# Attention heads of the first two batches re-staged in a fused attention and two-layer kernel on one core

## The chip, the core and the metric

The kernel runs on one core of a Trainium2 chip. A core has a matrix engine (TensorE; PE in the profile, with its weight loads as PEld), a vector engine (DVE), an activation engine (ACT), a third elementwise engine (POOL) and a sync engine (SP) whose queue here issues every transfer. Each engine works through its own instruction stream in order; semaphores hold an instruction until what it reads or overwrites is ready. The metric is the device time of one execution in microseconds. Before the change it was 974.35 us, the median of three runs between 972.32 and 974.64.

## What is computed

For 8 batches of 8 heads with 576 positions of 64 numbers each, windowed causal attention: heads 0 to 3 see the last 32 positions, heads 4 to 7 every fourth of the last 128. Its output, 4608 tokens of 512 numbers, goes through two dense layers of width 2048 with a piecewise quadratic activation between them. In short:

```python
scores = (q @ k.T) / 8                      # per batch and head
scores = where(mask_plain or mask_dilated, scores, -1e9)
attn = exp(scores - max) / (sum(exp(scores - max)) + 1e-9)
x = (attn @ v) as [4608, 512]
h = x @ w_in                                # 512 -> 2048
g = where(h >= 1, h, where(h <= -1, 0, (h + 1)**2 / 4))
out = g @ w_out                             # 2048 -> 512
```

## The kernel before

Heads are numbered n = 8 * batch + head. Dilated heads are permuted on the host, so every head becomes six diagonal tiles of 96 queries by 128 keys. For one pair of heads the work is: scores on PE (tiles s), then one fused DVE instruction per tile that adds the mask, scales, negates and takes the row minimum (`reduce`, 12 for a pair), softmax on the tile c (in place, 96 x 768 for a head), six PE transposes per head (tiles t) copied by ACT and DVE into pt, and 24 small matmuls with the values (tiles o, 12 for each half). The values are stored as token columns in two parts: ACT writes the rounded part xh, DVE the residue xl (`store_x`).

The dense layers work in split precision. A block of 512 tokens is t, a block of 128 hidden units is f: `layer1(t, f)` is 12 matmuls of 512 columns into h, followed by a clamp on DVE, a square on ACT, a maximum on DVE, a rounding on ACT (gh) and a residue on DVE (gl); `layer2(t, f)` is 12 matmuls of 512 columns into four accumulators acc0 to acc3. The main loop runs over steps s = (t, f), 144 of them, with layer 1 of step s and layer 2 of step s - 2.

The weights come as 64-bit numbers. `fetch` transfers a block; `weights` turns it into a rounded part and a residue: two ACT instructions (one for w_out), one or two on DVE (the shift of wo_raw, the combination wi_m or wo_m), an ACT rounding and a POOL subtraction. `behind(marks, ...)` lets the preparation of a block begin only after an ACT and a DVE instruction named by the marks. In step s the blocks wo s and wi s + 3 are prepared, behind the activation of step s - 2.

The attention stands in three places. The first batch (heads 0 to 7, four pairs) is computed ahead of the loop; its `softmax_first` subtracts the row extreme of the whole head on POOL, takes one exponential of 768 columns on ACT, and on DVE sums the rows, takes the reciprocal and multiplies. The second batch (heads 8 to 15) is put into slots of the loop, two slots per step: slot 2s stands between layer 1 and layer 2 of step s, slot 2s + 1 behind layer 2. Its `softmax` uses six exponentials per head on ACT, each with the bias and the row sum in the instruction, and multiplies on POOL. Pair n starts at slot u = 7 (n - 8) / 2 with scores at u and u + 1, transposes at u + 5 and u + 6, values at u + 7. So the values of one pair and the first scores of the next fall into the same slot. From head 16 on another form is used, from slot 27; the change leaves that part alone.

The order on PE and on SP is the order in which the code is written. On DVE, ACT and POOL a list scheduler with an engine model sets the order; `tc.high_priority(offset=...)` moves instructions ahead in its list. PSUM gives h two banks, the attention two banks (tag "att"), the accumulators four; while the accumulators are unused, heads below 8 take the four acc banks in turn for scores and transposes (`bank`). Some buffers of late weight blocks hold operands of the first batch, so their transfers cannot start before these are used up.

Of the kernel before, what the change touches and what calls it, by code (L numbers as in the profile page):

```python
# [19 lines left out]
F32 = mybir.dt.float32  # L21
# [4 lines left out]
ALU = mybir.AluOpType  # L26
# [16 lines left out]
def body(ctx, tc, q, k, q2, k2, v, mask, eye, w_in, w_out, out):  # L43
# [105 lines left out]
    def bank(n):  # L149

        if n >= H:
            return "att", 2
        turn[0] += 1
        return banks[(turn[0] - 1) % len(banks)]
# [23 lines left out]
    def scores_pair(n, t0, t1):  # L178
# [24 lines left out]
        for m, sv in zip(pair, svs):  # L203
            for t in range(t0, t1):
                which = (0 if t == 0 else 2) if plain else t % 3
                reduce(m, t, (sv[:, t - t0], msk[:, which]))
# [34 lines left out]
    def softmax(n):  # L241
        c, st = heads[n]["c"], heads[n]["st"]
        for t in range(NQ):
            nc.scalar.activation(  # L244
                out=c[:, t],
                in_=c[:, t],
                func=AF.Exp,
                bias=st[:, 0, t : t + 1],
                scale=-1.0,
                accum_out=st[:, 1, t : t + 1],  # L250
            )
        nc.vector.scalar_tensor_tensor(  # L252
            out=st[:, 1], in0=st[:, 1], scalar=EPS, in1=st[:, 1], op0=ALU.add, op1=ALU.max
        )
        nc.vector.reciprocal(out=st[:, 2], in_=st[:, 1])  # L255
        nc.gpsimd.tensor_tensor(  # L256
            out=c, in0=c, in1=st[:, 2].unsqueeze(2).broadcast_to([QT, NQ, 128]), op=ALU.mult
        )

    def softmax_first(n):  # L260

        c, st = heads[n]["c"], heads[n]["st"]

        def spread(a):
            return a.unsqueeze(2).broadcast_to([QT, NQ, 128])

# [3 lines left out]
        nc.vector.scalar_tensor_tensor(  # L270
            out=st[:, 1], in0=st[:, 1], scalar=EPS, in1=st[:, 1], op0=ALU.add, op1=ALU.max
        )
        nc.vector.reciprocal(out=st[:, 2], in_=st[:, 1])
        last["dve"] = nc.vector.tensor_tensor(out=c, in0=c, in1=spread(st[:, 2]), op=ALU.mult)  # L274
# [46 lines left out]
    def store_x(src, t, c, dst):  # L321
        xh, xl = xtile(t)
        last["act"] = nc.scalar.copy(out=dst(xh[:, c]), in_=src)
        last["dve"] = nc.vector.tensor_tensor(  # L324
            out=dst(xl[:, c]), in0=src, in1=dst(xh[:, c]).bitcast(F32), op=ALU.subtract
        )
# [43 lines left out]
    def layer1(t, f, cs=range(NC), bank=("h", 2)):  # L370
# [13 lines left out]
        if cs[-1] < NC - 1:  # L384
# [5 lines left out]
        nc.vector.tensor_scalar(  # L390
            out=y, in0=hp, scalar1=-1.0, scalar2=1.0, op0=ALU.max, op1=ALU.min
        )
        nc.scalar.activation(out=y, in_=y, func=AF.Square, bias=half_t, scale=0.5)  # L393

        activated = nc.vector.tensor_tensor(out=hp, in0=hp, in1=y, op=ALU.max)  # L395
        copied = nc.scalar.copy(out=gh, in_=hp)  # L396
        if t == 0:
            last["g", f] = copied, activated
        nc.vector.tensor_tensor(out=gl, in0=hp, in1=gh.bitcast(F32), op=ALU.subtract)  # L399
# [57 lines left out]
    for n in range(H, native, 2):  # L457
        u = 7 * (n - H) // 2
        place(u, lambda n=n: scores_pair(n, 0, 4))
        place(u + 1, lambda n=n: (scores_pair(n, 4, NQ), after_pair(n)))  # L460
# [32 lines left out]
    def pair(n):  # L493
        scores_pair(n, 0, 4)
        scores_pair(n, 4, NQ)
        softmax_first(n)
        softmax_first(n + 1)
# [23 lines left out]
    with tc.manual_schedule(engines={mybir.EngineType.PE, mybir.EngineType.SP}):  # L521
# [28 lines left out]
        early_values(6)  # L550
        behind(second, ("wi", 3))
# [3 lines left out]
        for s in range(len(steps) + lag):  # L555
            if s == 1:
                for f in range(9, NF):
                    fetch(f, w_in, "wi")
                    fetch(f - 2, w_out, "wo")
                fetch(NF - 2, w_out, "wo")  # L560
                fetch(NF - 1, w_out, "wo")
# [78 lines left out]
```

## Time and profile before

| what | value |
|---|---|
| median of 3 runs | 974.35 us |
| the profiled execution: its own time | 970.9 us |
| its span, first to last instruction | 968.9 us |
| mean granted PE clock | 0.978 of full |
| DVE, ACT, POOL busy | 738.7, 479.4, 231.4 us |
| from 200 us on | PE busy all but a few us |
| PE busy from 0 to 200 us | 167.6 us of 200 |

Span and waits come from one execution taken by the hardware profiler. A line of a timeline view gives start, duration, engine, code line, operation, output<-input, shape and, in brackets, how long the engine had been idle and what ended that. A line of the view of the chain of waits gives start, length and the work on the path that ended last. A line of the view of stages gives the busy time of each engine in a stretch, the granted PE clock, the share of the DMA engines and their rate. Durations in a timeline include a tail in which the next instruction already runs: successive starts are closer than the durations. The lines that matter are shown in the prediction.

### The profile page before, as it was taken

How to read it: one execution, taken by the hardware profiler on the slowest of the kernel's cores; microseconds unless marked ns; L12 is line 12 of the kernel's file. 1: busy time of each engine (PE TensorE's matmuls, PEld its weight loads, DVE VectorE, ACT ScalarE, POOL GpSimd, SP SyncE). 2: the span in 40 equal slices, each digit the busy share in tenths (PEclk: the TensorE clock that was granted, in tenths of full speed). 3: DMA queues.
4: the chain of work that ended last, by engine and by line, in shares of the span. 5: the costliest groups of instructions: out<-in, count | busy, mean ns of one | idle time of the engine just before them, and what ended most of it. 6: DMA issues, size and time to landing. Idle time of an engine off the chain costs nothing.

```text
span 968.9 us, 14398 instructions
## 1 busy us (share of the span) xinstructions
PE 930.3 (96%) x4822; PEld 751.9 (78%) x4822; DVE 738.7 (76%) x2043; ACT 479.4 (49%) x1291; POOL 231.4 (24%) x148
## 2 busy tenths in 40 slices
PE   6779978999999999999999999999999999999997
PEld 5657767888777888878888888888788888888886
DVE  7888666988898898989898889898988743334333
ACT  2677765555565555545555555555555432222222
POOL 3344333222222222222222222222222200000000
PEclk8779999999999999999999999999999999999999
DMA  9674100322232222322232223211322010001001
GB/s 348 239 275 156 43 1 26 111 67 68 68 90 84 59 58 64 110 68 67 67 111 67 67 66 94 60 64 57 109 68 83 1 44 1 0 1 44 1 1 44
DMA packets 31017, 73.85 MB, mean 76 GB/s; under 512 B 3520, under 2 KB 3808, under 8 KB 30944
## 3 DMA queue, kind: packets, MB, share of 16 engines
q1 hardware_dynamic: 30944, 72.94, 23.1%
q8 instruction: 38, 0.62, 0.3%
q14 instruction: 35, 0.29, 0.1%
HBM read 63.49 MB, written 9.44 MB: 75 GB/s over the span
## 4 chain that ended last, share of the span: by engine, by line
PE 82%; DVE 9%; ACT 6%; issue 2%; DMA 1%; SPq 0%; POOL 0%; ACTq 0%; DVEq 0%; POOLq 0%
PE h L377 37%; PE acc L412 37%; PE s L218 3%; PE o L339 3%; ACT c L244 2%; ACT y L393 1%; DVE pt L282 1%; DVE c L252 1%; DVE c L167 1%; DMA out<-out 1%; PE s L196 1%; DVE c L274 1%; DVE h L395 1%; DVE c L269 1%; DVE wi_m L124 1%
## 5 line engine op out<-in xcount | busy, mean ns | idle before, releaser
L412 PE MATMUL acc<-wo,gh 128*128 128x512 f32 x1152 | 384.7, 395 | 0.0
L377 PE MATMUL h<-xh,wi 128*128 128x512 f32 x1152 | 365.2, 398 | 3.6 <-DVE gl L399 3.3
L412 PEld LDWEIGHTS acc<-wo,gh 128*128 128x128 f32 x1152 | 216.6, 188 | 48.6 <-DVE out L422 0.4
L377 PEld LDWEIGHTS h<-xh,wi 128*128 128x128 f32 x1152 | 212.1, 191 | 47.0 <-DVE gl L399 3.5
L377 PE MATMUL h<-xl,wi 128*128 128x512 f32 x576 | 229.2, 398 | 0.0
L412 PE MATMUL acc<-wo,gl 128*128 128x512 f32 x576 | 225.3, 391 | 0.0
L244 ACT ACTIVATE c<-c 96x128 f32<-96x128 f32 x336 | 131.4, 392 | 149.5 <-DVE c L167 149.4
L141 POOL TENSOR_TENSOR kk<-kr,kk 128x608 fp32r<-128x608 f32 x48 | 95.1, 1981 | 417.1 <-ACT kk L137 417.1
L393 ACT ACTIVATE y<-y,consts 128x512 f32<-128x512 f32 x144 | 104.3, 724 | 162.2 <-DVE y L390 155.3
L395 DVE TENSOR_TENSOR h<-h,y 128x512 f32<-128x512 f32 x144 | 100.7, 700 | 64.6 <-ACT y L393 63.6
L390 DVE TENSOR_SCALAR y<-h 128x512 f32<-128x512 f32 x144 | 97.2, 675 | 54.1 <-PE h L377 54.0
L399 DVE TENSOR_TENSOR gl<-h,gh 128x512 fp32r<-128x512 f32 x144 | 98.7, 685 | 44.8 <-ACT gh L396 44.1
L377 PEld LDWEIGHTS h<-xl,wi 128*128 128x128 f32 x576 | 109.5, 190 | 26.1 <-DVE xl L324 0.4
L396 ACT CAST gh<-h 128x512 fp32r<-128x512 f32 x144 | 84.8, 589 | 83.5 <-PE acc L412 60.1
L412 PEld LDWEIGHTS acc<-wo,gl 128*128 128x128 f32 x576 | 108.5, 188 | 21.3
L282 DVE STREAM_TRANSPOSE pt<-c 32x192 f32<-32x192 f32 x288 | 105.9, 368 | 3.5
L256 POOL TENSOR_TENSOR c<-c 96x768 f32<-96x768 f32 x56 | 82.8, 1480 | 38.1 <-DVE c L255 35.3
L237 DVE TENSOR_TENSOR c<-s,msk 96x256 f32<-96x256 f32 (+1 forms) x168 | 61.4, 377 | 15.1 <-PE s L218 13.9
L167 DVE CUSTOM_DVE_ANT_0 c<-s,c 96x128 f32<-96x128 f32 x288 | 70.6, 281 | 1.1
L252 DVE SCALAR_TENSOR_TENSOR c<-c 96x6 f32<-96x6 f32 x56 | 64.4, 1150 | 7.9 <-ACT c L244 5.3
L218 PEld LDWEIGHTS s<-kk,qs 128*96 128x96 f32 x288 | 44.8, 161 | 23.9 <-issue 7.8
L244 ACT ACTIVATION_READ_ACCUMULATOR c<-c 96x1 f32 x336 | 63.1, 188 | 0.0
(51 smaller groups left out, 673.2 us busy)
## 6 DMA issues: line engine op xcount, KB each, us to landing
kr<-k_in SPq DMA_DIRECT2D x56, 304.0 KB, 3.4
qr<-q_in SPq DMA_DIRECT2D x56, 288.0 KB, 2.8
vt<-v_in SPq DMA_DIRECT2D x32, 384.0 KB, 4.0
out<-out SPq DMA_DIRECT2D x36, 256.0 KB, 3.1
wi_raw<-w_in SPq DMA_DIRECT2D x16, 512.0 KB, 9.1
wo_raw<-w_in SPq DMA_DIRECT2D x16, 512.0 KB, 9.6
msk<-mask_in SPq DMA_DIRECT2D x1, 144.0 KB, 3.7
ident<-eye_in SPq DMA_DIRECT2D x1, 36.0 KB, 5.1
```

What stands on the lines that cost most here:

```text
L141: nc.gpsimd.tensor_tensor(out=kk[:, 1], in0=hd["kr"], in1=kk[:, 0].bitcast(F32), op=ALU.subtract)
L167: nc.vector.tensor_tensor_reduce(out=heads[n]["c"][:, t], in0=parts[0], in1=parts[1], scale=-1.0 / 8.0, scalar=3.0e38, op0=ALU.add, op1=AL ...
L244: nc.scalar.activation(out=c[:, t], in_=c[:, t], func=AF.Exp, bias=st[:, 0, t : t + 1], scale=-1.0, accum_out=st[:, 1, t : t + 1],)
L256: nc.gpsimd.tensor_tensor(out=c, in0=c, in1=st[:, 2].unsqueeze(2).broadcast_to([QT, NQ, 128]), op=ALU.mult)
L282: nc.vector.transpose(out=pt[r : r + 32, :, 32 * g : 32 * g + 32], in_=c[32 * g : 32 * g + 32, :, r : r + 32],)
L377: PE.matmul(out=hp, lhsT=wi[f][:, w, 128 * c : 128 * c + 128], rhs=x[:, c], start=c == 0 and i == 0, stop=c == NC - 1 and i == len(terms) - 1,
L390: nc.vector.tensor_scalar(out=y, in0=hp, scalar1=-1.0, scalar2=1.0, op0=ALU.max, op1=ALU.min)
L393: nc.scalar.activation(out=y, in_=y, func=AF.Square, bias=half_t, scale=0.5)
L395: activated = nc.vector.tensor_tensor(out=hp, in0=hp, in1=y, op=ALU.max)
L396: copied = nc.scalar.copy(out=gh, in_=hp)
L399: nc.vector.tensor_tensor(out=gl, in0=hp, in1=gh.bitcast(F32), op=ALU.subtract)
L412: PE.matmul(out=acc[m], lhsT=g[:, r], rhs=wo[f][:, w], start=f == 0 and i == 0, stop=f == NF - 1 and i == len(terms) - 1,)
```

## The change

First batch. The pairs of heads 0 to 3 now use exponentials of 128 columns with bias and row sum in the ACT instruction (`exp`, six per head), and POOL multiplies. The pairs of heads 4 to 7 keep the whole-head form (`whole`), and of each pair one head is multiplied on POOL and one on DVE.

Second batch. The scores of heads 8 and 9 move ahead of the loop, in front of the second half of layer 1 of step 0, and use acc banks, as do the transposes of head 8. Pair n starts at slot u = 4 (n - 8) - 5, so that every slot holds one part: transposes of heads 8 and 9 in slots 0 and 1, values in slot 2, scores of 10 and 11 in slots 3 and 4, transposes in 8 and 9, values in 10, and so on by eight slots.

Transfers. The 15 weight transfers from wi 9 to wo 15 now stand in SP's queue ahead of the operands of heads 12 and 13, not behind them. Priorities: `reduce` of heads from 8 on, `store_x` and the activation of layer 1 are moved ahead in the scheduler's list.

```diff
     def bank(n):
-        if n >= H:
+        if n > H:
             return "att", 2
...
-        for m, sv in zip(pair, svs):
+        with tc.high_priority(offset=100 if n >= H else 0):
             for t in range(t0, t1):
-                which = (0 if t == 0 else 2) if plain else t % 3
-                reduce(m, t, (sv[:, t - t0], msk[:, which]))
+                for m, sv in zip(pair, svs):
+                    which = (0 if t == 0 else 2) if plain else t % 3
+                    reduce(m, t, (sv[:, t - t0], msk[:, which]))
...
+    def exp(n, t):
         c, st = heads[n]["c"], heads[n]["st"]
+        last["act"] = nc.scalar.activation(
+            out=c[:, t],
+            in_=c[:, t],
+            func=AF.Exp,
+            bias=st[:, 0, t : t + 1],
+            scale=-1.0,
+            accum_out=st[:, 1, t : t + 1],
+        )
...
+    def normalise(n, engine):
+        c, st = heads[n]["c"], heads[n]["st"]
+        last["dve"] = nc.vector.scalar_tensor_tensor(
             out=st[:, 1], in0=st[:, 1], scalar=EPS, in1=st[:, 1], op0=ALU.add, op1=ALU.max
         )
+        last["dve"] = nc.vector.reciprocal(out=st[:, 2], in_=st[:, 1])
+        done = engine.tensor_tensor(out=c, in0=c, in1=spread(st[:, 2]), op=ALU.mult)
...
+    def whole(n):
         c, st = heads[n]["c"], heads[n]["st"]
         nc.gpsimd.tensor_tensor(out=c, in0=c, in1=spread(st[:, 0]), op=ALU.subtract)
         last["act"] = nc.scalar.activation(out=c, in_=c, func=AF.Exp, scale=-1.0)
         nc.vector.tensor_reduce(out=st[:, 1], in_=c, op=ALU.add, axis=mybir.AxisListType.X)
...
     def store_x(src, t, c, dst):
         xh, xl = xtile(t)
+        with tc.high_priority(offset=60):
...
+        with tc.high_priority(offset=60):
+            nc.vector.tensor_scalar(
+                out=y, in0=hp, scalar1=-1.0, scalar2=1.0, op0=ALU.max, op1=ALU.min
+            )
...
     for n in range(H, native, 2):
-        u = 7 * (n - H) // 2
-        place(u, lambda n=n: scores_pair(n, 0, 4))
-        place(u + 1, lambda n=n: (scores_pair(n, 4, NQ), after_pair(n)))
+        u = 4 * (n - H) - 5
+        if n > H:
+            place(u, lambda n=n: scores_pair(n, 0, 4))
+            place(u + 1, lambda n=n: (scores_pair(n, 4, NQ), after_pair(n)))
...
     def pair(n):
         scores_pair(n, 0, 4)
         scores_pair(n, 4, NQ)
-        softmax_first(n)
-        softmax_first(n + 1)
+        if n < H // 2:
+            for t in range(NQ):
+                exp(n, t)
+                exp(n + 1, t)
+            normalise(n, nc.gpsimd)
+            normalise(n + 1, nc.gpsimd)
+        else:
+            whole(n)
+            whole(n + 1)
+            normalise(n, nc.gpsimd)
+            normalise(n + 1, nc.vector)
...
         early_values(6)
+        scores_pair(H, 0, 4)
+        scores_pair(H, 4, NQ)
+        for f in range(9, NF):
+            fetch(f, w_in, "wi")
+            fetch(f - 2, w_out, "wo")
...
+        after_pair(H)
         behind(second, ("wi", 3))
...
-            if s == 1:
-                for f in range(9, NF):
...
```

In three places the instruction streams show what moved. In names such as c4_221 the head (or block) comes first and a buffer number second; s, t, o are scores, transposes and values of a head. First POOL, in the first batch, from its first tile to the last. Before:

```order
L267 TENSOR_TENSOR c0_114<-c0_114 96x768
L267 TENSOR_TENSOR c1_127<-c1_127 96x768
L267 TENSOR_TENSOR c2_167<-c2_167 96x768
L267 TENSOR_TENSOR c3_169<-c3_169 96x768
L267 TENSOR_TENSOR c4_209<-c4_209 96x768
L267 TENSOR_TENSOR c5_211<-c5_211 96x768
L267 TENSOR_TENSOR c6_251<-c6_251 96x768
L267 TENSOR_TENSOR c7_253<-c7_253 96x768
```

and in the changed kernel (L276 subtracts, L264 multiplies):

```order
L264 TENSOR_TENSOR c0_114<-c0_114 96x768
L264 TENSOR_TENSOR c1_127<-c1_127 96x768
L276 TENSOR_TENSOR c4_221<-c4_221 96x768
L276 TENSOR_TENSOR c5_223<-c5_223 96x768
L264 TENSOR_TENSOR c2_173<-c2_173 96x768
L264 TENSOR_TENSOR c3_175<-c3_175 96x768
L276 TENSOR_TENSOR c6_263<-c6_263 96x768
L276 TENSOR_TENSOR c7_265<-c7_265 96x768
L264 TENSOR_TENSOR c4_221<-c4_221 96x768
L264 TENSOR_TENSOR c6_263<-c6_263 96x768
```

Eight subtractions became four subtractions and six multiplications; the multiplications of heads 2 and 3 stand behind the subtractions of heads 4 and 5.

Second PE, behind the second half of layer 1 of step 0. Before, two more layer blocks and a layer-2 block stand between the scores of head 8 and its transposes; in the changed kernel the transposes follow at once, then half a layer block, the values and the next scores:

```order
L310 MATMUL t8_0_648<-ident_65,c8_543 128x96 x4
L310 MATMUL t8_4_654<-ident_65,c8_543 128x96 x2
L310 MATMUL t9_0_658<-ident_65,c9_545 128x96 x4
L310 MATMUL t9_4_664<-ident_65,c9_545 128x96 x2
L382 MATMUL h0_1_514<-xh0_380,wi1_408 128x512 x2
L382 MATMUL h0_1_514<-xl0_381,wi1_408 128x512
...
L344 MATMUL o8_0_696<-pt0_67,vt8_325 64x96 x3
L344 MATMUL o8_0_696<-pt1_68,vt8_325 64x96 x3
L344 MATMUL o8_1_705<-pt0_67,vt8_325 64x96 x3
L344 MATMUL o8_1_705<-pt1_68,vt8_325 64x96 x3
L198 MATMUL s10_0_721<-kr10_332,qr10_331 96x128
L198 MATMUL s11_0_723<-kr10_332,qr10_331 96x128
```

The values of heads 8 and 9 and the scores of 10 and 11 came behind layer-2 block 1 before, about two and a half steps later; their neighbourhood (o8, then s10) is the same in both.

Third DVE, between the maximum of layer 1 of step 1 and the last residue of the values of head 8, in the changed kernel:

```order
L401 TENSOR_TENSOR h0_1_514<-h0_1_514,y0_1_688 128x512
L123 TENSOR_SCALAR wo_raw3_339<-wo_raw3_339 128x512
L126 SCALAR_TENSOR_TENSOR wi_m5_747<-wi_m5_747,wi_raw5_337 128x512
L329 TENSOR_TENSOR xl1_394<-o8_0_696,xh1_393 128x288
L329 TENSOR_TENSOR xl1_394<-o8_1_705,xh1_393 128x160
L405 TENSOR_TENSOR gl0_1_690<-h0_1_514,gh0_1_689 128x512
L126 SCALAR_TENSOR_TENSOR wo_m3_823<-wo_m3_823,wo_raw3_339 128x512
L126 SCALAR_TENSOR_TENSOR wi_m6_830<-wi_m6_830,wi_raw6_341 128x512
L329 TENSOR_TENSOR xl2_715<-o8_1_705,xh2_714 128x128
```

Before, only one weight instruction stood between the residues of these values; now the last of them stands behind a residue of layer 1 and two weight instructions.

More of the change, by code (lines that the diff above doesn't have):

```diff
@@ L239, in scores_split, with spread, softmax @@
                 reduce(n, t, (sv[:, t - t0, 0], c[:, t]))
-    def softmax(n):
+    def exp(n, t):
         c, st = heads[n]["c"], heads[n]["st"]
[L243 to L252, printed above, removed]
+        last["act"] = nc.scalar.activation(
[6 more added lines that the diff above has]
+        )
+    def spread(a):
+        return a.unsqueeze(2).broadcast_to([QT, NQ, 128])
+    def normalise(n, engine):
+        c, st = heads[n]["c"], heads[n]["st"]
+        last["dve"] = nc.vector.scalar_tensor_tensor(
             out=st[:, 1], in0=st[:, 1], scalar=EPS, in1=st[:, 1], op0=ALU.add, op1=ALU.max
         )
[L255 to L260, printed above, removed]
+        last["dve"] = nc.vector.reciprocal(out=st[:, 2], in_=st[:, 1])
+        done = engine.tensor_tensor(out=c, in0=c, in1=spread(st[:, 2]), op=ALU.mult)
+        if engine is nc.vector:
+            last["dve"] = done
+    def softmax(n):
+        for t in range(NQ):
+            exp(n, t)
+        normalise(n, nc.gpsimd)
+    def whole(n):
         c, st = heads[n]["c"], heads[n]["st"]
-        def spread(a):
-            return a.unsqueeze(2).broadcast_to([QT, NQ, 128])
         nc.gpsimd.tensor_tensor(out=c, in0=c, in1=spread(st[:, 0]), op=ALU.subtract)
@@ L269, in softmax_first @@
         nc.vector.tensor_reduce(out=st[:, 1], in_=c, op=ALU.add, axis=mybir.AxisListType.X)
[L270 to L274, printed above, removed]
     def transpose(n):
@@ L322, in store_x @@
         xh, xl = xtile(t)
[L323 to L326, printed above, removed]
+        with tc.high_priority(offset=60):
+            last["act"] = nc.scalar.copy(out=dst(xh[:, c]), in_=src)
+            last["dve"] = nc.vector.tensor_tensor(
+                out=dst(xl[:, c]), in0=src, in1=dst(xh[:, c]).bitcast(F32), op=ALU.subtract
+            )
     def values(n):
@@ L389, in layer1 @@
         gl = pool.tile([128, TOK], F32R, tag="gl", name=f"gl{t}_{f}", bufs=2)
[L390 to L399, printed above, removed]
+        with tc.high_priority(offset=60):
+            nc.vector.tensor_scalar(
+                out=y, in0=hp, scalar1=-1.0, scalar2=1.0, op0=ALU.max, op1=ALU.min
+            )
+            nc.scalar.activation(out=y, in_=y, func=AF.Square, bias=half_t, scale=0.5)
+            activated = nc.vector.tensor_tensor(out=hp, in0=hp, in1=y, op=ALU.max)
+            copied = nc.scalar.copy(out=gh, in_=hp)
+            if t == 0:
+                last["g", f] = copied, activated
+            nc.vector.tensor_tensor(out=gl, in0=hp, in1=gh.bitcast(F32), op=ALU.subtract)
         gs[t, f] = gh, gl
@@ L495, in pair @@
         scores_pair(n, 4, NQ)
-        softmax_first(n)
-        softmax_first(n + 1)
+        if n < H // 2:
+            for t in range(NQ):
+                exp(n, t)
+                exp(n + 1, t)
[4 more added lines that the diff above has]
+            whole(n + 1)
+            normalise(n, nc.gpsimd)
+            normalise(n + 1, nc.vector)
     def early_transposes(n):
@@ L550, in body @@
         early_values(6)
+        scores_pair(H, 0, 4)
[3 more added lines that the diff above has]
+            fetch(f - 2, w_out, "wo")
+        fetch(NF - 2, w_out, "wo")
+        fetch(NF - 1, w_out, "wo")
+        after_pair(H)
         behind(second, ("wi", 3))
@@ L555, in body @@
         for s in range(len(steps) + lag):
-            if s == 1:
-                for f in range(9, NF):
[L558 to L561, printed above, removed]
             if 0 < s < NF:
```

## The prediction

> **What bounds the kernel now.** I read the page first.
>
> ```profile
> span 968.9 us, 14398 instructions
> PE 930.3 (96%) x4822; PEld 751.9 (78%) x4822; DVE 738.7 (76%) x2043; ACT 479.4 (49%) x1291; POOL 231.4 (24%) x148
> ```
>
> PE is busy 96% of the span. Where the rest is, the stages tell:
>
> ```profile
> 15.00:25.00 10.00, 6.18 (x36) 4.66 (x36) 10.00 (x55) 3.03 (x6) 4.48 (x4) 0.50 1.03 405
> 25.00:35.00 10.00, 6.72 (x60) 5.84 (x60) 10.00 (x24) 6.82 (x14) 1.31 (x1) 0.66 1.03 407
> 42.00:50.00 8.00, 7.70 (x60) 5.42 (x58) 4.47 (x10) 4.96 (x13) 3.74 (x3) 1.00 0.00 0
> 60.00:70.00 10.00, 6.70 (x28) 5.28 (x27) 9.81 (x14) 7.42 (x15) 7.04 (x6) 0.80 1.02 412
> 500.00:600.00 100.00, 100.00 (x527) 81.11 (x526) 89.47 (x257) 53.53 (x160) 27.61 (x16) 1.00 0.25 76
> ```
>
> Columns: stretch, length, busy PE, PEld, DVE, ACT, POOL, clock, DMA share, GB/s. From 200 us on PE is the bound (100.00 of 100); nothing the change touches lies there, so what is won or lost earlier reaches the end one to one. From 15 to 35 us DVE is (10.00 of 10, twice), and ACT has room. Between lie PE's waits; for 47 to 170 us:
>
> ```profile
> PE s L196 <- DVE xl L324: 4.5, 4, 1.7
> PE s L196 <- issue: 3.3, 1, 3.3
> PE h L377 <- DVE gl L399: 3.3, 1, 3.3
> PE s L196 <- DVE c L167: 2.2, 2, 1.9
> PE s L218 <- DVE xl L324: 2.1, 1, 2.1
> PE t L306 <- ACT pt L308: 1.5, 1, 1.5
> PE s L218 <- DVE pt L308: 0.5, 1, 0.5
> ```
>
> Total, times, longest. The rows "s <- xl" are scores that want the PSUM banks which the values just ahead of them have not left. After a wait PE is slow, too; from the chain of waits:
>
> ```profile
> 67.32 5.50 PE h L377 x12
> 81.34 2.99 PE h L377 x12
> 84.94 2.94 PE acc L412 x12
> 106.78 1.91 PE s L196 x14
> 108.68 3.69 PE acc L412 x12
> 137.37 2.20 PE s L196 x16
> 80.25 1.08 PE s L196 x14
> 139.56 3.67 PE h L377 x12
> ```
>
> Twelve matmuls take 5.50 us right after a wait of 3.3 us and 2.99 undisturbed.
>
> **First batch, up to T0.** Groups of instructions up to 37 us (line, engine, operation, count, busy us, mean ns, idle before), single rows of the timeline, and two of the chain, whose x8 and x12 count an accumulator read with each instruction (0.21 us per reduced tile, 0.38 us per exponential):
>
> ```profile
> L267 POOL TENSOR_TENSOR c<-c 96x768 f32<-96x768 f32 x8 | 11.5, 1467 | 14.3 <-DVE c L167 12.5 <-DVE c L270 1.8
> L274 DVE TENSOR_TENSOR c<-c 96x768 f32<-96x768 f32 x8 | 7.5, 943 | 0.0
> L269 DVE TENSOR_REDUCE c<-c 96x6 f32<-96x768 f32 x8 | 7.3, 921 | 0.0
> L270 DVE SCALAR_TENSOR_TENSOR c<-c 96x6 f32<-96x6 f32 x8 | 2.8, 351 | 0.0
> 23.42 2.90 POOL L267 TENSOR_TENSOR c<-c 96x768 f32<-96x768 f32 x2 [4.31 <-DVE c L167]
> 24.62 0.17 DVE L273 RECIPROCAL c<-c 96x6 f32<-96x6 f32 x1
> 24.95 1.38 DVE L270 SCALAR_TENSOR_TENSOR c<-c 96x6 f32<-96x6 f32 x1
> 34.80 0.94 DVE L274 TENSOR_TENSOR c<-c 96x768 f32<-96x768 f32 x1
> 48.68 0.21 DVE L324 TENSOR_TENSOR xl<-o,xh 128x32 fp32r<-128x32 f32 x1 [0.16 <-ACT xh L323]
> 20.27 0.84 DVE c L167 x8
> 55.38 2.29 ACT c L244 x12
> ```
>
> I mark two points. T0, when the last residue of heads 6 and 7 is stored, is 48.9 us (row 48.68). M, when layer-1 block 4, layer-2 block 1 and all scores of heads 10 and 11 are done, is 84.9 (row 84.94 starts there).
>
> DVE loses 4 of the 8 row sums and 6 of the 8 multiplications: 4 x 0.92 + 6 x 0.94 = 9.3 us of durations, about 8.5 since starts are some 8% closer. ACT gains 24 exponentials, 24 x 0.38 = 9.2 us, where it has room, but DVE catches up with them: 36 reductions of 0.21 and 0.7 us of small instructions are 8.3, so it waits 0.9 us before the division term of head 2. One residue and two copies, 0.85 us, fall behind the last multiplication that stood ahead of it. So 8.5 - 0.9 - 0.85 = 6.75 us, less what DVE waits for POOL.
>
> That is the unknown. The tiny 96x6 instruction at 24.95 lasted 1.38 us and ended with POOL's second subtraction (24.87 to 26.32); the reciprocal beside the first took its usual 0.17. POOL now runs ten instructions of 1.45 us almost back to back instead of eight with gaps. In its new order the division term of head 2 meets the subtraction of head 4 (0.7 us), that of head 3 the subtraction of head 5 (1.3), that of head 4 the subtraction of head 7 (0.8): 2.8 us. Before, such waits cost 2.8 - 8 x 0.13 = 1.75, which also go. Bounds: no waits at all, 6.75 + 1.75 = 8.5 earlier; waits of 5.6 us, twice the walk, 2.9 earlier. The walk gives 5.7; a contact that just misses a boundary costs one more instruction, so I take the middle of the walk and the late end, **4.4 us**: T0 = 44.5.
>
> A rule that speaks against the change: where POOL already multiplies head 4 when DVE multiplies head 5, DVE would stand still for that multiplication, 1.47 us by the first row. The Trainium skill, "SBUF — State Buffer", section "Who interferes with whom", says that a DVE instruction with two SBUF inputs contends with a POOL instruction that reads SBUF, that whichever starts first holds the shared ports for its whole length, and that tensor_reduce never contends. The 1.38 us agree; no row shows a DVE multiplication of that size that meets one of POOL.
>
> **Second batch, T0 to M.** Rows that price the new order:
>
> ```profile
> 39.23 0.56 ACT wi_m L113
> 38.64 0.35 ACT pt L308
> 41.29 0.52 ACT wi L129
> 87.33 1.47 POOL L256 TENSOR_TENSOR c<-c 96x768 f32<-96x768 f32 x1 [5.05 <-DVE c L255]
> 76.05 1.43 PE L339 MATMUL o<-pt,vt 128*64 128x96 f32 x24
> 121.61 3.03 DVE L124 SCALAR_TENSOR_TENSOR wi_m<-wi_m,wi_raw 128x512 uint32<-128x512 uint32 x1
> ```
>
> Times from T0, all engines:
>
> - The scores of 8 and 9 are done, since they use free acc banks. DVE reduces 12 tiles in 2.5 us, ACT ends 12 exponentials at 5.0 (head 8 at 4.2), POOL multiplies head 8 by 5.9, head 9 by 7.5 (1.47 each). PE, with layer 1 of step 0 done, waits for both: transposes at 5.9 and 7.5. Behind them on PE stand half of layer 1 of step 1, o8 and s10; the activation of step 1 and through it the weights of step 3 wait for these.
> - Behind the exponentials ACT has the square of step 0 (5.6), its rounding (7.1), five weight instructions (5 x 0.56, 9.9), and only then the two copies of the transposes (2 x 0.35, 10.6). The values o8 run from 10.7 to 12.2 (1.43).
> - ACT goes on: three roundings of 0.52 (12.2), square 1, wi_m5, first xh (13.7). DVE: shift of wo_raw3, wi_m5, two residues, gl, wo_m3, wi_m6, the last residue. Without contact with POOL it is through at 17.2, when ACT has delivered the last xh (16.9). But POOL has three weight subtractions from 11.25 to 15.1 and the next from 16.6; shift, wi_m5 and wo_m3 meet them (a wi_m beside POOL took 3.03 us): 19.5.
> - So s11 starts at 19.5 (bounds 17.2 and 21.5, one more contact of POOL's length on each side). 16 scores at slow clock 2.2, layer 1 of step 2 about 5.0, eight scores 0.6, then four blocks of 2.9: M = T0 + 38.9.
>
> Before, M - T0 was 84.9 - 48.9 = 36.0. The change **loses 2.9 us** here (0.6 to 4.9), though PE stands still for some 11 us of it: the old order loses there too (the 3.3, 2.2 and about 2.3 of the wait rows, and the slow 5.50). M would be 83.4.
>
> **From M to 170 us.** Of PE's waits, those before M are gl 3.3, c 2.2 and half the first row, 2.3; what is left is 3.3 + 2.2 + 2.1 + 1.5 and a 0.5: 9.6 us. The slow stretches add 3.69 - 2.94, 3.67 - 2.99 and for the two sets of scores about 0.8 and 1.0: 3.2. Sum 12.8. In the new slots 12 matmuls (2.9 us) stand between the values and the next scores: xh, residues, square and maximum are through some 3.2 us after the first value, and the scores come at 1.43 + 2.9 = 4.3. If POOL holds the shift between the residues, up to 1.3 us shows, per pair. I keep 1.5 us (0 to 5): **gain 11.3**.
>
> **Transfers.** From 42 to 50 us nothing moved (share 0.00), later the queue ran full (1.02): weight blocks behind blocked operands.
>
> ```profile
> wi_raw<-w_in SPq DMA_DIRECT2D x16, 512.0 KB, 9.1
> ```
>
> They are used a block per step, much later, and no wait row of PE names a transfer. In SP's queue block wi 12 waits for the values of heads 6 and 7 to leave its buffer, near T0, and holds the eight blocks and the operands of head 12 behind it. Costed at nothing: 15 x 0.52 MB at 407 GB/s are 20 us, so the operands of head 12 still land before 70 us, and its scores come after 90. The priorities move nothing behind the last slot of the second batch.
>
> **Sum.** -4.4 + 2.9 - 11.3 = -12.8 us. The profiled execution's own time is 970.9 (span 968.9), 3.45 below the median; I take the difference from the median: 974.35 - 12.8 = **961.5 us**. Extremes: -8.5 + 0.6 - 12.8 = -20.7 (953.6) and -2.9 + 4.9 - 7.8 = -5.8 (968.5).
>
> **Rivals.**
>
> 1. *No contact on DVE and POOL.* T0 by 8.5 earlier, s11 at T0 + 17.2: -8.5 + 0.6 - 11.3 = -19.2, 955.1. For it: many 96x6 instructions took 0.15. Against: POOL has fewer gaps. 0.13.
> 2. *The first batch's gain is hidden.* Transfers run at a share of 1.03 up to 35 us; if a weight or operand bounds T0, only 2.9 - 11.3 = -8.4 is left: 966.0. Against: DVE's 10.00. 0.17.
> 3. *DVE's multiplication of head 5 waits out POOL's of head 4*: T0 later by 1.47, 963.0. 0.06. It is what the rule of the Trainium skill above, "SBUF — State Buffer", section "Who interferes with whom", would do here.
> 4. *The new waits eat it.* PE's two new waits (t8, s10) grow, because ACT and DVE do weights first: s11 at T0 + 30 would take 10.5 more: 972.0, within 0.3%. 0.08.
> 5. *Slower: weight preparation becomes the bound.* Each step needs three DVE instructions that can meet POOL. From 60 to 70 us DVE was busy 9.81 of 10 and PE 6.70. The section from T0 to 167 us is 118 us, of which some 23 are waits and slow stretches; its 95 us of PE work at 0.67 would take 142: +24, less the 4.4 won ahead, 994. It decides once PE's share there falls below 95 / 122.4 = 0.78. Against: the same weights per step from 90 on left PE busy, and four steps per pair instead of three and a half thin the rest out. 0.06.
>
> **How the numbers follow.** Forecast 0.50, rivals 0.13, 0.17, 0.06, 0.08, 0.06. A measurement of this kernel can tell about 0.3%, 2.9 us, from no change. Faster by more: 0.50 + 0.13 + 0.17 + 0.06 = 0.86; within: 0.08; slower: 0.06. Range 953 to 968.5: both extremes of the sum; it takes in the first three rivals.
>
> **What would show it.** Right: the last DVE multiplication of the first batch near 30 us, not 34.80; a gap of about 5 us before the transposes of head 8 and one of about 7 before the scores of 11, the latter ended by a residue; M near 83; no waits over 1 us for residues after it. 96x6 instructions above 1 us would confirm the contacts. Wrong: a wait for a transfer or for a weight subtraction, or DVE full beyond 60 us with PE below 0.78.

## The result, and the profile after

The changed kernel takes 956.87 us, the median of four runs between 956.14 and 957.85; the kernel before took 973.34 beside it. The ratio is 0.9837, with a 95% interval of 0.9808 to 0.9867: faster by 16.5 us, where 12.8 were forecast. The profiled execution has an own time of 957.35 us and a span that is 13.3 us shorter than before's 968.9:

```profile
span 955.6 us, 14440 instructions
PE 924.7 (97%) x4822; PEld 749.4 (78%) x4822; DVE 732.5 (77%) x2033; ACT 484.1 (51%) x1335; POOL 233.9 (24%) x150
```

Of the 13.3 us, 5.6 are PE's busy time (930.3 before) for the same 4822 matmuls, at a mean granted clock of 0.982 (0.978 before), and 7.7 are idle time.

The first batch, in the timeline of the changed kernel on DVE (start, length, engine, line, operation):

```profile
23.36 0.82 DVE L260 SCALAR_TENSOR_TENSOR c<-c 96x6 f32<-96x6 f32 x1
24.77 2.27 DVE L264 TENSOR_TENSOR c<-c 96x768 f32<-96x768 f32 x1
29.91 2.07 DVE L264 TENSOR_TENSOR c<-c 96x768 f32<-96x768 f32 x1
46.97 0.22 DVE L329 TENSOR_TENSOR xl<-o,xh 128x32 fp32r<-128x32 f32 x1 [0.17 <-ACT xh L328]
```

and on POOL:

```profile
24.76 1.47 POOL L264 TENSOR_TENSOR c<-c 96x768 f32<-96x768 f32 x1 [0.60 <-DVE c L263]
29.70 1.47 POOL L264 TENSOR_TENSOR c<-c 96x768 f32<-96x768 f32 x1 [3.48 <-DVE c L260]
```

The last multiplication begins at 29.91 us, before at 34.80. But both multiplications of VectorE, 0.94 us undisturbed, began within 0.21 us of one on POOL and took 2.27 and 2.07. T0, the last residue of heads 6 and 7, came at 47.2 us; before it was 48.9.

The first reduction of the kernel began at 6.90 us, before at 6.40, though the code ahead of it is the same: the eleven idle multiplications at the start took 4.90 us here and 4.40 before. In the fourteen profiled executions of this study the first reduction begins between 6.40 and 7.58 us. So times of two profiles can be shifted against each other by half a microsecond or more. Counted from the first reduction, T0 is 40.3 us against 42.5 before, a gain of 2.2.

On PE the second half of the values of heads 2 and 3 waits for a residue that stands among these instructions of VectorE, before for 3.14 us:

```profile
37.22 0.43 PE L339 MATMUL o<-pts_xh,vt 128*64 128x96 f32 x3 [3.14 <-DVE xl L324]
```

and in the changed kernel for 4.92:

```profile
34.44 0.74 PE L344 MATMUL o<-pts_xh,vt 128*64 128x96 f32 x3 [4.92 <-DVE xl L329]
```

The second batch, PE's waits from 47 to 170 us (total, times, longest), and the chain of waits of the changed kernel around M:

```profile
PE t L310 <- POOL c L264: 6.5, 2, 5.8
PE s L198 <- DVE xl L329: 5.5, 2, 2.9
```

```profile
67.22 1.99 PE s L198 x14
69.21 5.09 PE h L382 x12
74.30 0.61 PE s L198 x8
83.38 2.80 PE h L382 x12
```

Eight kinds of wait before (the prediction shows the seven longest), two now. The two stand between 47 and 68 us: transposes of heads 8 and 9 for POOL, scores of 10 and 11 for residues. M comes at 86.0 us, 1.1 later than before. Behind it PE waits for nothing up to 170 us. Two stretches of the view of stages, before

```profile
85.00:125.00 40.00, 37.84 (x200) 30.53 (x201) 30.39 (x76) 27.98 (x72) 17.88 (x13) 0.96 0.16 51
125.00:170.00 45.00, 37.60 (x218) 29.93 (x218) 29.58 (x82) 28.45 (x76) 15.54 (x11) 0.96 0.05 14
```

and after:

```profile
85.00:125.00 40.00, 39.95 (x248) 31.77 (x247) 32.27 (x76) 32.22 (x78) 18.87 (x14) 1.00 0.08 26
125.00:170.00 45.00, 45.00 (x235) 36.22 (x232) 37.75 (x102) 30.44 (x85) 17.83 (x12) 1.00 0.13 37
```

PE went from 75.4 busy of 85 us to 84.95, and the granted clock from 0.96 to 1.00. The first output transfer starts at 173.8 us instead of 185.8.

### The profile page after: what moved, and what is told of

The parts are those of the page before. It is cut to its first block, busy times and chain, and to the rows that moved or that the text cites. A ratio compares the mean times of both kernels' runs of the same rounds, so it can differ in the third digit from the quotient of the medians.

```text
span 955.6 us, 14440 instructions
## 1 busy us (share of the span) xinstructions
PE 924.7 (97%) x4822; PEld 749.4 (78%) x4822; DVE 732.5 (77%) x2033; ACT 484.1 (51%) x1335; POOL 233.9 (24%) x150
## 4 chain that ended last, share of the span: by engine, by line
PE 90%; DVE 4%; ACT 3%; DMA 2%; issue 1%; SPq 0%; ACTq 0%; DVEq 0%
PE h L382 40%; PE acc L418 40%; PE o L344 4%; PE s L221 4%; ACT c L246 2%; DVE c L260 1%; DMA wo_raw<-w_in 1%; PE s L198 1%; DMA kr<-k_in 1%; PE t L310 1%; PE s L195 1%; DVE pt L286 0%; ACT y L399 0%; DVE c L278 0%; DVE c L169 0%
## 5 line engine op out<-in xcount | busy, mean ns | idle before, releaser
L246 ACT ACTIVATE c<-c 96x128 f32<-96x128 f32 x360 | 140.5, 392 | 148.4 <-DVE c L169 148.4
L264 POOL TENSOR_TENSOR c<-c 96x768 f32<-96x768 f32 x62 | 91.3, 1475 | 63.8 <-DVE c L263 57.8
L260 DVE SCALAR_TENSOR_TENSOR c<-c 96x6 f32<-96x6 f32 x64 | 69.5, 1085 | 8.8 <-ACT c L246 6.2
L246 ACT ACTIVATION_READ_ACCUMULATOR c<-c 96x1 f32 x360 | 67.7, 188 | 0.0
```

The lines of the kernel that those rows point to most:

```text
L246: last["act"] = nc.scalar.activation(out=c[:, t], in_=c[:, t], func=AF.Exp, bias=st[:, 0, t : t + 1], scale=-1.0, accum_out=st[:, 1, t : t ...
L264: done = engine.tensor_tensor(out=c, in0=c, in1=spread(st[:, 2]), op=ALU.mult)
```

## The experiments

The theory to be tested: the gain lies in the matmuls that now stand between a pair's values and the next scores; the first batch brings less than 2 us because VectorE and GpSimd stand in each other's way; the new waits from 47 to 68 us cost nearly 3; fetches bring nothing. The rivals are the other shares of the change.

**One part alone.** First the first batch's softmax, with all else as before:

```diff
-        softmax_first(n)
-        softmax_first(n + 1)
+        if n < H // 2:
+            for t in range(NQ):
+                exp_first(n, t)
+                exp_first(n + 1, t)
+            normalise(n, nc.gpsimd)
+            normalise(n + 1, nc.gpsimd)
+        else:
+            whole(n)
+            whole(n + 1)
+            normalise(n, nc.gpsimd)
+            normalise(n + 1, nc.vector)
```

> The kernel before with the first batch's softmax on three engines alone; the second batch's slots, the fetches and the priorities stay as they were. Theory (nearly all of the gain comes from the slots): the last residue of heads 6 and 7 comes about 1.7 us earlier than before's 48.9 us, the stretch of the second batch keeps its waits, so the time falls by 0 to 3 us (970 to 973 us against before's 973). Rival 1 (the softmax brings half of the gain or more): 965 us or less. Rival 2 (the standing DVE multiplications eat it, and a longer stretch behind it takes back more): 974 us or more.

Measured 970.0 us against 973.55, ratio 0.9961 (0.9944 to 0.9978), 3.5 us. In its profile:

```profile
47.51 0.22 DVE L355 TENSOR_TENSOR xl<-o,xh 128x32 fp32r<-128x32 f32 x1 [0.17 <-ACT xh L354]
```

T0 at 47.7 us, 1.2 earlier than before (40.3 counted from the first reduction, as with the whole change), and the waits from 85 to 170 us are the old ones, row for row. A share of the gain and no more; neither rival holds.

Then the slots alone, with the old softmax, the fetches in their old place and no priorities:

```diff
-        if n >= H:
+        if n > H:
             return "att", 2
-        u = 7 * (n - H) // 2
+        u = 4 * (n - H) - 5
...
         early_values(6)
+        scores_pair(H, 0, 4)
+        scores_pair(H, 4, NQ)
+        after_pair(H)
```

> The kernel before with the second batch's slots alone (scores of heads 8 and 9 ahead of the loop, the other pairs' scores in slots of their own, the second batch's two buffers from head 10 on); the old softmax of the first batch, the fetches behind the first block and no priorities. Theory: the waits of TensorE at scores for residues after about 85 us go (13 us of the profile), and the stretch up to there loses some 1 to 3 us more than it did: 960 to 963 us. Rival 1 (the slots need the earlier first batch to be of use): over 966 us. Rival 2 (the softmax is worth nothing at all): 957 us, as the whole change.

Measured 959.4 us against 973.55, ratio 0.9861 (0.9846 to 0.9876): 14.2 us, a little more than expected. From 85 to 170 us its list of waits is empty. The two parts alone sum to 17.7 us, the whole change brought 16.5: nothing is left over for fetches and priorities. The fetches, 16 by the code (15 in the text above), were put back:

```diff
-        for f in range(9, NF):
-            fetch(f, w_in, "wi")
...
+            if s == 1:
+                for f in range(9, NF):
+                    fetch(f, w_in, "wi")
...
```

> The changed kernel with the block of weight fetches put back behind the first block's operands (issued in the second step of the loop). Theory (the transfers cost and bring nothing, since no weight is used within 20 us of landing): within 1 us of the changed kernel, 956 to 958 us. Rival (the order of fetches is part of the gain): 959 us or more. Second rival (fetching early pushed the first batch's operands back): 955 us or less, with the last residue of heads 6 and 7 earlier than 47.2 us.

Measured 957.4 us, ratio 0.9841, a span of 955.6 as with the change, and the scores of 11 start at 67.21 as there: the transfers bring nothing. The priorities were not tried alone.

**What between values and scores.** Each pair's scores from head 10 on, one slot earlier:

```diff
-            place(u, lambda n=n: scores_pair(n, 0, 4))
-            place(u + 1, lambda n=n: (scores_pair(n, 4, NQ), after_pair(n)))
+            place(u - 1, lambda n=n: scores_pair(n, 0, 4))
+            place(u, lambda n=n: (scores_pair(n, 4, NQ), after_pair(n)))
```

> The changed kernel with each pair's first scores from head 10 on one slot earlier, directly behind the values of the pair before, as most of them stood before the change; nothing else is moved. Theory (the 13 us come from the 12 matmuls that stand between values and scores): waits of scores for residues of about 1.5 to 2.5 us come back for the pairs 12 and 14 and with them a slower clock in their blocks: 961 to 966 us. Rival (the gain comes from four slots per pair and the emptier VectorE, not from what stands between): the time stays within 1.5 us of 957.

Measured 966.7 us, just above the 961 to 966 of the theory, ratio 0.994 (0.992 to 0.9959): 9.8 us of the gain are gone through one slot. Its waits from 85 to 170 us:

```profile
PE s L198 <- issue: 2.9, 1, 2.9
PE s L198 <- DVE xl L329: 2.2, 2, 1.7
PE t L310 <- DVE pt L312: 0.2, 1, 0.2
```

The first two are of the kind and size that before's list has (3.3 and 2.2). The slower clock that I expected with them did not come: from 85 to 170 us it was 1.00 here. PE was busy 79.5 of these 85 us, against 84.95, and the transposes of head 10 came 2.1 us later: 7.6 of the 7.9 us by which the span is longer. So the theory holds for the waits, and they cost without a slow clock too. Of the 16.5 us, 9.8 go with this slot and 3.5 with the softmax alone; what the other 3 or so hang on (four slots for a pair, the scores of heads 8 and 9 ahead of the loop) no run takes apart.

**The first batch's contacts.** Heads 5 and 7 multiplied on GpSimd as well:

```diff
             normalise(n, nc.gpsimd)
-            normalise(n + 1, nc.vector)
+            normalise(n + 1, nc.gpsimd)
```

> The changed kernel with the multiplications of heads 5 and 7 by their reciprocals on GpSimd too, so that no 96x768 multiplication runs on VectorE. Theory (VectorE stood still in the 2.27 and 2.07 us multiplications because GpSimd was in one of its own): no VectorE instruction over 1.4 us is left between 20 and 50 us, the residues of heads 2 to 5 come up to 4 us earlier, the last residue of heads 6 and 7 at 44 to 45.5 us instead of 47.2; the time falls by 0.5 to 2.5 us, to 954.5 to 956.5. Rival (GpSimd is now the series that sets the end: four multiplications of 1.45 us in a row): the last residue at 47 us or later and the time 957 us or more.

Measured 957.5 us, ratio 0.9836: no change, and the theory was wrong. The rival's numbers came (T0 at 47.4 us), but not its reason. VectorE's timeline shows why:

```profile
28.92 1.92 DVE L126 SCALAR_TENSOR_TENSOR wi_m<-wi_m,wi_raw 128x512 uint32<-128x512 uint32 x1
31.03 2.90 DVE L126 SCALAR_TENSOR_TENSOR wi_m<-wi_m,wi_raw 128x512 uint32<-128x512 uint32 x1
47.14 0.21 DVE L329 TENSOR_TENSOR xl<-o,xh 128x32 fp32r<-128x32 f32 x1 [0.18 <-ACT xh L328]
```

GpSimd multiplied in a row from 28.83 us, and two weight combinations, 0.68 us in the changed kernel, met it and took 1.92 and 2.90, the second beside the rest of a multiplication and a weight subtraction of GpSimd that followed it at 32.13. The standing had only moved to the next instruction with two inputs. The opposite edit takes GpSimd's multiplications away:

```diff
-            normalise(n, nc.gpsimd)
+            normalise(n, nc.vector)
             normalise(n + 1, nc.vector)
```

> The changed kernel with the multiplications of heads 4 to 7 all on VectorE, so that GpSimd has no multiplication beside VectorE's second half of the first batch. Theory (VectorE's two-input instructions stand still behind GpSimd's, whichever they are; with heads 5 and 7 on GpSimd the standing had moved to two weight instructions, 1.92 and 2.90 us): four multiplications of about 0.94 us, weight instructions of about 0.68, the last residue of heads 6 and 7 at 45.5 to 46.7 us instead of 47.2, the time 955.5 to 957.0. Rival (the long multiplications have another cause, such as operands that come late): some of the four take over 1.5 us still, and the last residue is at 47 us or later.

Measured 955.5 us, ratio 0.9822 (0.9784 to 0.986); T0 at 45.8 us, 1.4 earlier than with the change (1.2 counted from the first reduction).

```profile
24.40 1.81 DVE L264 TENSOR_TENSOR c<-c 96x768 f32<-96x768 f32 x2
28.96 0.95 DVE L264 TENSOR_TENSOR c<-c 96x768 f32<-96x768 f32 x1
30.46 0.94 DVE L264 TENSOR_TENSOR c<-c 96x768 f32<-96x768 f32 x1
31.33 1.28 DVE L126 SCALAR_TENSOR_TENSOR wi_m<-wi_m,wi_raw 128x512 uint32<-128x512 uint32 x2
```

Four multiplications at their price, and the weight combinations too. VectorE has two multiplications more than in the changed kernel and is through earlier. The median moved as T0 did, by 1.4 us, but the intervals of the two ratios overlap: the shorter multiplications are shown, the gain in time is only likely. That VectorE's instructions with two inputs stand behind GpSimd's is the rule cited in the prediction from the Trainium skill, "SBUF — State Buffer", section "Who interferes with whom"; the three traces agree with it. The row sums agree too: in the changed kernel they keep their 0.94 us (from 21.10 and 22.23) beside GpSimd's subtractions (21.26 to 24.16).

**The new waits from 47 to 68 us.** The weight preparation of the second and third step held back (`last["pt", ...]` keeps the copies of the transposes):

```diff
+            last["pt", t0 > 0] = done
...
-                behind(last["g", max(s - 2, 0)], *todo)
+                if s > 1:
+                    behind(last["g", s - 2] if s > 2 else marks(), *todo)
...
             run(2 * s + 1)
+            if s == 0:
+                behind((last["pt", False], last["pt", True]), ("wo", 1), ("wi", 4))
```

> The changed kernel with the weight preparation of the loop's second step behind the copies of the transposes of head 9 and that of the third step behind the residues of heads 8 and 9. Theory (from 47 to 86 us the new waits come from ScalarE and VectorE doing weights ahead of copies and residues): the scores of head 11 start 3 to 5 us earlier than 67.2 us, the mark M (last of four half-clock blocks before TensorE is without waits) moves from 86 to 81.5 to 83.5, the time is 952.5 to 954.5. Rival (the half granted clock after the wait for head 8's scores sets that stretch, not the weights): the scores of 11 at 66 us or later and the time within 1 us of the changed kernel's 957. Second rival (the weights come late then and become the wait): waits for wo or wi appear and the time is over 958.

Measured 953.0 us, ratio 0.98 (0.9769 to 0.9832). PE's timeline, scores of 10 and of 11:

```profile
61.95 0.46 PE L198 MATMUL s<-kr,qr 64*96 64x128 f32 x2 [1.58 <-DVE xl L330]
63.06 1.99 PE L198 MATMUL s<-kr,qr 64*96 64x128 f32 x14 [0.66 <-DVE xl L330]
```

The scores of 11 come at 63.06 instead of 67.22 (0.4 of it the earlier start) and M at 81.8, and the time falls by 3.9 us, as the theory had it. The other wait, that of the transposes of head 8, stays (6.1 us). It is the aim of the next:

```diff
+        scores_pair(H, 0, 4)
+        scores_pair(H, 4, NQ)
         layer1(0, 0, range(2))
         layer1(0, 1, range(2))
         early_values(6)
-        scores_pair(H, 0, 4)
-        scores_pair(H, 4, NQ)
```

> The changed kernel with the scores of heads 8 and 9 in front of the two first halves of layer 1, so that 24 more matmuls lie between them and their transposes. Theory (the 5.8 us wait of the transposes of head 8 is the length of reductions, exponentials and multiplication behind scores that come too late): the wait falls to 1.5 to 3.5 us, the time is 953 to 956. Rival (VectorE has no room for the reductions ahead of the residues of heads 6 and 7): the last residue is later than 47.2 us by as much as the wait shrinks, and the time is within 1 us of 957.

Measured 954.2 us, ratio 0.9811 (0.9779 to 0.9843): 2.7 us. From PE's timeline:

```profile
51.30 1.17 PE L382 MATMUL h<-xh,wi 128*128 128x512 f32 x2 [3.27 <-ACT xh L328]
53.48 2.12 PE L310 MATMUL t<-ident,c 96*128 96x96 f32 x12
```

The wait of the transposes is gone altogether, but more than half of it came back one step ahead: layer 1 now waits 3.27 us for the rounding of heads 6 and 7, which stands behind twelve exponentials on ACT; T0 moved to 53.3 us, far later than 47.2 (0.7 of it the later start). So the rival was right that T0 would be late by about the wait that went, and wrong on the time, which still fell.

**Together.** The three edits in one kernel:

```diff
-            normalise(n, nc.gpsimd)
+            normalise(n, nc.vector)
...
+        scores_pair(H, 0, 4)
+        scores_pair(H, 4, NQ)
         layer1(0, 0, range(2))
...
+                behind((last["pt", False], last["pt", True]), ("wo", 1), ("wi", 4))
```

> The changed kernel with all three together: heads 4 to 7 multiplied on VectorE, the weight preparation of the second and third steps held back, the scores of heads 8 and 9 in front of the two half blocks. Theory (the three take time from three different waits): the gains of 1.4, 3.9 and 2.7 us add up to 8.0, 949 us (948 to 950.5). Rival (two of them shorten the same wait, and what one takes the other no longer finds): no better than the best alone with the smaller one, 951.5 us or more.

Measured 951.0 us, ratio 0.9776 (0.9759 to 0.9794), between the two expectations: 5.9 of the 8.0 us. Layer 1's wait for the rounding is now 4.4 us, and the second half of the values of heads 2 and 3 waits 4.3. (By the order of the code it is these; the next expectation calls them the values of heads 4 and 5.) These two were the aim of one more step:

```diff
-        behind(scored, ("wi", 0), ("wi", 1))
         early_transposes(4)
         early_values(2)
         first = marks()
+        behind(first, ("wi", 0), ("wi", 1))
```

> The one before, and the preparation of the first two weight blocks of layer 1 behind the residues of heads 2 and 3 instead of the scores of heads 6 and 7. Theory (the two weight instructions on VectorE, 1.28 us together, and four on ScalarE stand ahead of the residues for which the values of heads 4 and 5 wait): the wait of these values, 3.9 us with the multiplications on VectorE, falls by 1 to 1.5 us and the time by as much. Rival (the two blocks are then late for layer 1, whose first half block follows within 7 us): a wait of layer 1 for wi appears and the time is the same or more than without it.

Measured **946.6 us**, ratio 0.9726 (0.9709 to 0.9743), the fastest kernel of this study: 10 us less than the change, 26 less than before. The edit was worth 4.4 us where I expected 1 to 1.5. Among its waits:

```profile
PE t L310 <- POOL c L264: 4.3, 1, 4.3
PE s L198 <- DVE xl L330: 4.3, 2, 2.3
PE o L345 <- DVE c L263: 1.8, 1, 1.8
PE h L383 <- ACT wi L131: 0.9, 1, 0.9
PE h L383 <- ACT xh L329: 0.9, 1, 0.9
PE h L383 <- POOL wi L132: 0.9, 1, 0.9
```

The second half of the values of heads 2 and 3 waits 1.8 us instead of 4.3 (the row "o <- DVE c"). The rival was right that layer 1 then waits for the two blocks, twice 0.9 us; but the wait for the rounding fell from 4.4 to 0.9 as well, which neither expectation had. The scores of heads 8 and 9 now come 3.6 us earlier, and eight of the twelve exponentials, all of which stood ahead of the rounding, are through by 41.2 us; with the three edits alone they began at 44.2. The first row is the wait of transposes in the first batch, which none of the edits shortened.

**The slow clock behind a wait.** Idle multiplications of a constant in front of the transposes of head 8, in the changed kernel:

```diff
             tp = ps.tile([128, 512], F32, tag=tag, name=f"t{n}_{t0}", bufs=bufs)
+            if n == H and t0 == 0:
+                half = half_t.broadcast_to([128, 128])
+                for _ in range(12):
+                    PE.matmul(out=tp[:, :128], lhsT=half, rhs=half, start=True, stop=True)
```

> The changed kernel with twelve idle multiplications of a constant (as the eleven at its start, 0.45 us each there) in front of the transposes of head 8, written into the bank that these overwrite: 5.35 us of work of TensorE in a wait of 5.83. Theory (a wait of some microseconds brings the half granted clock, 0.50 in the stretch from 50 to 60 us, and it is this that makes the work behind it slow): the granted clock stays at 1.00 through that wait and behind it, the blocks up to the scores of head 10 take about half, the time falls by 1 to 3 us, to 954 to 956. Rival (the clock falls for another reason, such as what other engines do): the stretch keeps its 0.50, the idle multiplications take twice as long and push the transposes back: 959 us or more. Second rival (the work behind the wait is hidden anyway, since the scores of 10 and 11 wait for ScalarE and VectorE): the clock stays up and the time is within 1 us of 957.

Measured 954.0 us, ratio 0.9818 (0.9795 to 0.984), 2.8 us less, but not for the reason I gave. The stages of the changed kernel (the third column from the right is the granted clock):

```profile
48.00:50.00 2.00, 0.00 (x0) 0.00 (x0) 2.00 (x19) 2.00 (x11) 0.00 (x0) 0.97 1.03 420
58.00:60.00 2.00, 2.00 (x12) 1.25 (x13) 1.54 (x3) 2.00 (x6) 0.94 (x1) 0.50 1.03 401
```

and of the kernel with idle multiplications:

```profile
52.00:53.00 1.00, 0.00 (x0) 0.00 (x0) 1.00 (x1) 0.52 (x1) 1.00 (x1) 0.89 1.02 410
58.00:60.00 2.00, 2.00 (x19) 1.35 (x19) 1.31 (x3) 2.00 (x5) 1.20 (x1) 0.60 1.03 395
```

The twelve took 2.94 us, not 5.35, since those at the kernel's start, which I had taken for the price, go at half of this pace. So half of the wait was left, and the half clock came all the same, 3 us later. The gain is from another place: the list scheduler, with the new matmuls in its model, put a residue of heads 8 and 9 ahead of a weight combination. On VectorE, in the changed kernel

```profile
61.77 1.76 DVE L126 SCALAR_TENSOR_TENSOR wi_m<-wi_m,wi_raw 128x512 uint32<-128x512 uint32 x1
63.45 0.67 DVE L329 TENSOR_TENSOR xl<-o,xh 128x288 fp32r<-128x288 f32 x2
```

and with idle multiplications:

```profile
61.51 0.67 DVE L333 TENSOR_TENSOR xl<-o,xh 128x288 fp32r<-128x288 f32 x2
62.11 1.17 DVE L126 SCALAR_TENSOR_TENSOR wi_m<-wi_m,wi_raw 128x512 uint32<-128x512 uint32 x1
```

The scores of 10 start at 62.01 instead of 63.95 and those of 11 at 64.82 instead of 67.22, though the transposes of head 8 were only 0.24 us earlier, as was the first reduction. That is what holding the weights back does, found by accident. The layer-1 block behind them took 4.4 us instead of 5.1, since the half clock there ended at 69.8 us instead of 73.8; so some 0.7 of the 2.8 us are clock after all, behind another wait than the one that was filled. The same with nine of them in the fastest kernel:

```diff
+            if n == H + 2 and t0 == 0:
+                half = half_t.broadcast_to([128, 128])
+                wp = ps.tile([128, 512], F32, tag="acc3", name=f"warm{m}")
+                for _ in range(5 if m == n else 4):
+                    PE.matmul(out=wp[:, :128], lhsT=half, rhs=half, start=True, stop=True)
```

> The fastest kernel so far (946.6 us: multiplications on VectorE, weights held back, scores of 8 and 9 early) with nine idle multiplications in front of the scores of heads 10 and 11, written into a bank that layer 2 takes later: 4.0 us of work of TensorE in two waits of 2.35 and 1.90 us. Theory: the half granted clock behind them (0.50 from 56 to 62 us) does not come, the 14 scores take 1.0 instead of 1.99 us and the next layer-1 block 2.9 instead of 4.9: 943 to 945 us. Rival (the clock falls all the same): 946.5 us or more.

Measured 946.7 us, against 946.6 without: the rival's number. The half clock came all the same, but in its profile it lasts from 56.4 to 59.8 us instead of 56.0 to 62.8, and the layer-1 block behind the scores of 11 takes 3.6 us instead of 5.0 (58.42 to 62.03, without them 58.32 to 63.36). The times show no difference; in this execution layer 1 waited longer for its first two blocks, 2.0 and 1.2 us. Of the two waits the first was filled, of the second 1.7 us were left. Whether a wait that is filled to its end would keep the clock up is left open.

## Why the prediction was right, and where not

- **The end.** 961.5 us were forecast with a range of 953 to 968.5; 956.9 lies inside, 4.6 us below the forecast. In the profile's own terms the sum was -12.8 us and the span fell by 13.3. The parts are not as close.
- **T0, -4.4 forecast, -1.7 measured: the step that failed.** The division terms met GpSimd as walked (0.82, 1.29 and 0.82 us against 0.7, 1.3 and 0.8). What failed first is that rival 3, given 0.06 and one contact, came true at both multiplications that VectorE kept: 1.33 and 1.13 us. Its mechanism was right; for head 7 the prediction names no contact. That the last multiplication began near 30 us, as forecast, is partly luck, since the first of these contacts is in it. What failed second is PE's part, put at nothing: behind the longer wait (4.92 us instead of 3.14) its clock was 0.50 from 34 to 38 us, and the values that had waited, the transposes of heads 6 and 7 and the values of heads 4 and 5 took 5.7 us instead of 4.9. And the start came 0.5 us later, by chance. From the walk's 5.7 us, 2.5 for the contacts, 0.8 for PE and 0.5 for the start leave 1.9; 1.7 were measured. That the contacts hold T0 back is shown by the kernel that multiplies heads 4 to 7 on VectorE alone: 45.8 us, in spite of two multiplications more.
- **T0 to M, 38.9 forecast, 38.8 measured.** The scores of 11 began 20.0 us behind T0 (19.5), ended by a residue as walked; the gap of about 7 us came as two, 2.93 before the scores of 10 and 2.53 before those of 11. From there to M it was 18.8 us (19.4), so the close sum is two small misses that cancel. That the weight work ahead of copies and residues sets this, and not the slow clock, the held-back weights show: 4.2 us earlier.
- **From M on, 11.3 forecast, 13.0 measured up to the first output transfer.** The wait and slow rows of before, 12.8 us, went entirely; the 1.5 us that I kept for residues did not appear. Another 1.4 us came behind 290 us; of these the rows of waits behind 170 us give 0.6, the rest is open.
- **From the profile to the median, the other step that failed.** I took the difference of the two profiled executions from the median. Before's profiled execution was a quick one: its span is 968.9 us, and 32 of the 39 executions of before beside the experiments are longer (967.2 to 974.2). Its first reduction is the earliest of the fourteen profiled. The spans fall as the granted clock rises: the longest has 0.974, the three with 0.982 have 967.2 to 968.0. The changed kernel's profiled execution is not a quick one (957.35, its median 956.87). So some 3 of the 16.5 us come from the execution that I took for the kernel; how much of them is slow clock is not shown.
- **Rivals.** Rival 1 (no contact) fell with the rows of 2.27 and 2.07. Rival 2 (a transfer bounds T0) fell too: the changed kernel's chain of waits from its first matmul to 44.6 us holds no transfer, and T0 moved when only multiplications moved. That no wait row of PE names a transfer holds for 47 to 170 us; near 8 us one does, 1.3 us before and 0.7 with the change. Rival 4's waits came, but at their walked size. Rival 5 did not come: VectorE had 70 busy of 85 us from 85 us on, with PE at 84.95.

## What to carry to other kernels

Between the matmuls that fill a PSUM bank and those that want it next, let there be as much other work of the matrix engine as the emptying takes; here one slot, 12 matmuls, was worth 9.8 us. Before an engine is relieved by sharing its work with another, look whether both can run at once: the relief moved the standing from one instruction to the next, and only taking the second engine away removed it. And work without a near deadline (weights needed steps later) is to stand behind what the matrix engine waits for on each engine; holding it back was worth 3.9 us and 4.4 in two places.

## What the runs showed of the hardware

- A VectorE instruction with two inputs in SBUF that starts beside a GpSimd one grows by the rest of it and sometimes by the next one too: 0.94 to 2.27 us beside one of 1.47, 0.68 to 2.90 beside the rest of one and the next. A shift with one input (`wo_raw`, 0.42 us) took 1.42 beside a multiplication of GpSimd. GpSimd stands as well: with heads 5 and 7 on it, one of its multiplications took 1.91 us instead of 1.47, behind the VectorE instruction of 1.92.
- The half granted clock comes on a grid: in all fourteen traces the stretches between two changes of the clock last whole multiples of 3.41 us. Its onset behind an idle TensorE varies: 2.2 us (idle from 47.64, half from 49.9), 2.0 with idle multiplications (idle from 50.78, half from 52.8), 3.3 in the first batch (idle from 29.5, half from 32.8) and 4.5 in the kernel before (idle from 34.1, half from 38.6, though it had worked again from 37.2). It outlasts the idle time: PE worked again at 53.5, and the clock was back at 60.1. The Trainium skill, "TensorE: Matmul & The Clock Gate", section "Part 1: The HAM clock gate", says that the clock is halved after an idle window of about 3.4 us whose phase runs freely. The traces agree with the length and the free phase; but in the 3.41 us up to 49.9 TensorE had still worked for 1.2 us (46.5 to 47.6), so the window need not be wholly idle.
- At the kernel's start the stages give a clock of 1.00, yet the idle multiplications go at half of their later pace. Each has two passes: in the kernel before these start 0.21 us apart up to 4.5 us and 0.11 us apart from there on, and the first entry of the clock in its trace stands at 4.5 us; in the changed kernel they are 0.21 apart throughout, and the first entry stands at 5.5. So eleven took 4.90 us, 0.45 each, and twelve later 2.94 us, 0.245 each.
